# Raw weights of an attention and MLP kernel: two tiles of a chunk and two assembled ones, or six of half a chunk converted in place

## Chip, core and metric

The kernel runs on one core of one Trainium2 chip. The metric is the device time of one execution in microseconds (us), the median of three runs. The core has five instruction streams that are named by their engines: PE (TensorE, matmuls), DVE (VectorE), ACT (ScalarE), POOL (GpSimd) and SP (SyncE, which here only asks for DMA transfers). ACT also asks for some transfers, in the same stream as its arithmetic.

## What is computed

Top-k attention over 4 batches of 8 heads, 576 positions and a head size of 64, then two MLPs on all 2304 tokens.

```python
scores = scale * np.matmul(q, k.transpose(0, 1, 3, 2))
kth = np.partition(scores, -32, axis=-1)[..., -32:-31]
scores = np.where(scores >= kth, scores, -1000000000.0)
attn = softmax(scores)                      # exp(s - max) / (sum + 1e-09)
x = matmul(attn, v)                         # to [2304, 512]
...
h = np.maximum(x @ w_in, 0.0)               # 512 -> 2048
x = h * h @ w_out                           # 2048 -> 512
...
h = x @ w_in2
out = np.maximum(0.01 * h, h) @ w_out2
```

The kernel gets q, k, v and the weights as 64-bit words; it makes fp32 values of them itself. For matmuls it splits each operand into a high and a low part and sums three products (high by high, high by low, low by high).

## The kernel before

**Attention** keeps DVE busy: per row tile four rounds of MAX8 and MATCH_REPLACE8 find the 32nd largest score (L928, L930). ACT makes exponentials and copies banks of PSUM, POOL does the low parts, PE scores, transposes and products.

**The MLPs** work on blocks of 512, 256, 384, 512, 256 and 384 tokens. A phase is one block in one layer, and has 16 steps; step f uses chunk f of the layer's weights: 512 words of w_in and 512 of w_out in each of 128 partitions, as 64-bit words 1 MB. Per step PE makes h (12 matmuls, L653), ACT `ga` and `gh` (L663, L664 in layer 0; L670, L672 in layer 1), POOL the low part `gl`, and PE adds to `acc` (12 matmuls of 512 columns, L690 or L692).

**Fresh chunks.** In the first phase of each layer (32 steps, both for block 0) a chunk comes from the inputs. `w_raw` loads it (L522, SP) into a raw tile of 8 KB a partition (tag `wraw`, two tiles). `w_convert` turns it into fp32, two steps ahead of its use, in the pieces that STAGES spreads over a step: ACT takes the low 32-bit words of the whole chunk to a tile of their own, `wc` (L543; 4 KB a partition, two tiles), then for each half ACT moves the scaled high words to a bank of PSUM with Prelu, whose large slope for negative numbers marks the sign (L552), DVE shifts and ORs them into `wc` (L559), ACT copies the result as the high part to `wi` or `wo` (L563), and POOL subtracts for the low part (L564). `w_store` writes `wi` and `wo` to DRAM for the later phases (two transfers per chunk, SP), which read them back with `w_load`. The raw tile is free once both halves were marked, `wc` once POOL has subtracted.

**Chunks 0 and 1** are loaded and prepared early, by `lead_passes` (low words L583 at 26 to 30 us, high words L584) and `lead_bits` at the end of block 0's attention. They use Copy for the high words, and so a second DVE operation for the sign (L590, L591).

**Output.** At the end of a layer-1 phase ACT copies each `acc` to a tile `y` (L708; same tag and two tiles as `wc`), and asks for the transfers to the output (L710) in its own queue. Block 5's input takes the two `wraw` tiles.

**Order.** A scheduler sets each engine's order from the order in which the program writes the instructions and from priorities (`high_priority`, `behind`); tiles of a tag are handed out in turn or as they come free, and whoever writes a tile waits for the readers of what stood in it. Of the MLPs, `run_moe` runs quanta of three matmuls between the attention's slots.

Of the kernel before, what the change touches and what calls it, by code (L numbers as in the profile page):

```python
# [57 lines left out]
WRB = 2  # L58
WCB = 2
# [28 lines left out]
def topk_attention_moe_moe2_kernel(  # L88
# [323 lines left out]
    def block_x(blk):  # L412

        if "x" not in blk:
            i = SETS[blk["idx"]]
            m = max(x["n"] for x in blocks if SETS[x["idx"]] == i)
            if i == 2:
                ts = [pool.tile([P, 2, 2, m], R, tag="wraw", name="x2", bufs=WRB) for _ in range(NK // 2)]
                blk["x"] = [(t[:, i, 0], t[:, i, 1]) for t in ts for i in range(2)]
# [96 lines left out]
    def w_raw(i):  # L516
        if i >= len(steps) or not fresh[i]:
            return
        _, layer, f = steps[i]
        if W64:  # L520
            t = pool.tile([P, 1024, 2], U, tag="wraw", name="wraw", bufs=WRB)
            SP.dma_start(t.rearrange("p c t -> p (c t)"), WS[layer][f].bitcast(U))  # L522
        else:
            t = pool.tile([P, 1024], F, tag="wraw", name="wraw", bufs=WRB)
            SP.dma_start(t, WS[layer][f])
        wraw[i] = t
# [9 lines left out]
    def w_convert_steps(i):  # L536
# [4 lines left out]
        if W64:  # L541
            b = pool.tile([P, 1024], U, tag="wc", name="wc", bufs=WCB)
            ACT.activation(b, raw[:, :, 0], AF.Copy, scale=L_SCALE, bias=L_BIAS)  # L543
            c = b.bitcast(F)
        else:
            c = raw
        v = [None, None]

        def high(x):
            if W64:  # L550
                v[x] = bank()
                ACT.activation(v[x], raw[:, x * 512:x * 512 + 512, 1].bitcast(F), AF.Prelu, scale=H_SCALE,  # L552
                               alpha=2.0 ** 32)

        def bits(x):
            if W64:
                vu, bx = v[x].bitcast(U), b[:, x * 512:x * 512 + 512]
                with behind("dve"):
                    DVE.scalar_tensor_tensor(bx, vu, 3, bx, op0=OP.logical_shift_left, op1=OP.bitwise_or)  # L559

        def parts(x):
            w, cx = w2[x], c[:, x * 512:x * 512 + 512]
# [11 lines left out]
    def lead_passes(i):  # L574
        led[i] = []
        raw = wraw.pop(i)
        c = pool.tile([P, 1024], U, tag="wc", name="wc", bufs=WCB)
        for x, w in enumerate(w_alloc(i)):
            xs = slice(x * 512, x * 512 + 512)
            lo, hi, b = raw[:, xs, 0], raw[:, xs, 1], c[:, xs]  # L580
# [423 lines left out]
```

## Time and profile before

| | us |
|---|---|
| median of three runs | 1190.59 (1190.24 to 1194.26) |
| the profiled execution | 1191.68 |
| its span in the trace | 1189.9 |
| busy: PE, DVE, ACT, POOL | 1127.2, 840.9, 818.9, 748.5 |

The rows further down are of that profiled execution, 1.1 us above the median. Starts are counted from the start of the span. In square brackets a timeline gives how long an engine sat idle before an instruction, and what released it. The stretches are: attention alone to 165 us; to 195 the step over to the first MLP block; to 395 the two fresh phases, with a seam between the layers at 300 to 330; then phases that reload their weights, with attention beside them to about 930; then MLPs alone.

### The profile page before, as it was taken

The numbers are of one execution on the slowest core, as the hardware profiler recorded it, in microseconds if no ns is written. First come the engines' busy times: TensorE is split into PE (matmuls) and PEld (weight loads), VectorE is DVE, ScalarE is ACT, GpSimd is POOL, SyncE is SP. The second block draws the span as 40 slices with busy tenths as digits, with TensorE's granted clock in tenths as the row PEclk, the third lists the DMA queues.
The fourth block names the chain that finished last, engine by engine and source line by source line (L and its number), as shares of the span: only waits on it lengthen the run. The fifth ranks groups of instructions, "written<-read, shape, count | busy, mean of one in ns | idle before, by whom it ended". The sixth has DMA issues, their size and how long they took to land.

```text
span 1189.9 us, 20032 instructions
## 1 busy us (share of the span) xinstructions
PE 1127.2 (95%) x6376; PEld 991.7 (83%) x6376; DVE 840.9 (71%) x1771; ACT 818.9 (69%) x1823; POOL 748.5 (63%) x960
## 2 busy tenths in 40 slices
PE   5898977999899999999999999999999999999997
PEld 4777766778678899999998997888788899999996
DVE  7999998766775759999999998999998100110010
ACT  6999988998989768877776776566866433333322
POOL 7968747999779677677897766777756443002100
PEclk9899989999899999999999998999999999999999
DMA  9868757998999697899897886777675499779973
GB/s 311 281 215 284 255 196 259 383 344 309 328 349 331 211 349 269 281 330 384 303 307 255 302 297 231 224 238 229 201 238 184 158 333 323 259 247 346 352 260 120
DMA packets 108201, 329.53 MB, mean 277 GB/s; under 512 B 17216, under 2 KB 25408, under 8 KB 104000
## 3 DMA queue, kind: packets, MB, share of 16 engines
q1 hardware_dynamic: 105472, 323.53, 79.1%
q10 hardware_dynamic: 2624, 4.72, 1.1%
q8 instruction: 52, 0.85, 0.3%
q14 instruction: 53, 0.43, 0.1%
HBM read 257.03 MB, written 71.17 MB: 276 GB/s over the span
## 4 chain that ended last, share of the span: by engine, by line
PE 73%; ACT 11%; DVE 8%; DMA 4%; issue 2%; POOL 2%; SPq 0%; ACTq 0%; POOLq 0%; DVEq 0%
PE h L653 30%; PE acc L692 16%; PE acc L690 13%; PE att L447 5%; DVE m L928 4%; PE att L350 3%; DVE w L930 3%; PE att L436 2%; ACT e L333 2%; PE att L310 1%; PE sp L310 1%; ACT s L311 1%; ACT stage L311 1%; ACT e L329 1%; DMA out_dram<-y 1%
## 5 line engine op out<-in xcount | busy, mean ns | idle before, releaser
L653 PE MATMUL h<-xh,wi 128*128 128x512 f32 (+2 forms) x1280 | 348.1, 346 | 6.0 <-ACT xh L704 2.8
L928 DVE MAX8 m<-w 128x8 f32<-128x576 f32 x432 | 312.8, 749 | 2.4
L653 PEld LDWEIGHTS h<-xh,wi 128*128 128x128 f32 x1280 | 228.6, 192 | 31.2 <-ACT ga L663 3.3
L673 POOL TENSOR_TENSOR gl<-ga,gh 128x512 fp32r<-128x512 f32 (+2 forms) x160 | 162.6, 1019 | 131.4 <-ACT gh L672 109.7
L930 DVE MATCH_REPLACE8 w<-m,w 128x576 f32<-128x576 f32 x288 | 213.3, 743 | 0.4
L653 PE MATMUL h<-xl,wi 128*128 128x512 f32 (+2 forms) x640 | 206.3, 342 | 0.0
L358 POOL TENSOR_TENSOR PTs<-whole,PTs 128x512 fp32r<-128x512 f32 x112 | 144.5, 1297 | 59.8 <-ACT whole L357 58.2
L690 PE MATMUL acc<-gh,wo 128*128 128x512 f32 (+2 forms) x768 | 156.9, 344 | 1.6 <-ACT y L708 0.8
L692 PE MATMUL acc<-wo,gh 128*128 128x512 f32 x576 | 152.5, 397 | 0.2 <-ACT gh L672 0.2
L690 PEld LDWEIGHTS acc<-gh,wo 128*128 128x128 f32 x768 | 128.2, 191 | 14.2 <-ACT gh L664 1.3
L329 ACT ACTIVATE e<-s,m 128x576 f32<-128x576 f32 x144 | 112.1, 781 | 39.8 <-DVE m L928 29.3
L653 PEld LDWEIGHTS h<-xl,wi 128*128 128x128 f32 x640 | 120.8, 190 | 10.7
L928 DVE MAX8 m<-s 128x8 f32<-128x576 f32 x144 | 104.3, 748 | 30.9 <-ACT s L311 28.5
L673 DVE TENSOR_TENSOR gl<-ga,gh 128x384 fp32r<-128x384 f32 x32 | 17.9, 559 | 151.2 <-ACT gh L672 148.5
L670 ACT ACTIVATE ga<-h 128x512 f32<-128x512 f32 (+2 forms) x96 | 46.5, 490 | 111.3 <-PE h L653 111.0
L692 PEld LDWEIGHTS acc<-wo,gh 128*128 128x128 f32 x576 | 105.1, 188 | 20.5 <-ACT gh L672 0.4
L333 ACT ACTIVATE e<-e,nb 128x576 f32<-128x576 f32 x144 | 111.5, 778 | 3.0 <-POOL nb L323 2.6
L930 DVE MATCH_REPLACE8 w<-m,s 128x576 f32<-128x576 f32 x144 | 107.0, 744 | 0.5
L350 PE MATMUL att<-ident,e 128*128 128x128 f32 x576 | 87.8, 277 | 7.7 <-ACT e L333 6.2
L447 PE MATMUL att<-PTs,VT 128*128 128x256 f32 (+2 forms) x504 | 89.4, 301 | 5.5 <-ACT whole L357 1.9
L665 POOL TENSOR_TENSOR ga<-ga 128x512 f32<-128x512 f32 (+2 forms) x80 | 66.4, 831 | 42.5 <-ACT gh L664 41.9
L345 POOL TENSOR_SCALAR e<-e,rc 128x576 f32<-128x576 f32 x112 | 83.0, 753 | 14.0 <-DVE rc L341 11.4
(100 smaller groups left out, 2070.3 us busy)
## 6 DMA issues: line engine op xcount, KB each, us to landing
wi<-wd SPq DMA_DIRECT2D x160, 512.0 KB, 5.2
wo<-wd SPq DMA_DIRECT2D x160, 512.0 KB, 5.2
wraw<-in_w_dram SPq DMA_DIRECT2D x32, 1024.0 KB, 7.6
sd<-stage SPq DMA_DIRECT2D x76, 288.0 KB, 3.0
s<-sd SPq DMA_DIRECT2D x76, 288.0 KB, 4.9
wd<-wi SPq DMA_DIRECT2D x32, 512.0 KB, 6.9
wd<-wo SPq DMA_DIRECT2D x32, 512.0 KB, 7.1
vd<-VT SPq DMA_DIRECT2D x16, 640.0 KB, 6.9
```

The costliest lines, as they stand in the source:

```text
L329: ACT.activation(t["e"], t["s"], AF.Prelu, bias=pr["m8"][:, i, 31:32], scale=-1.0, alpha=1.0 / FAR)
L333: ACT.activation(e, e, AF.Exp, bias=pr["nb"][:, i:i + 1], scale=-FAR, accum_out=pr["sum"][:, i:i + 1])
L345: POOL.tensor_scalar(e, e, pr["rc"][:, i:i + 1], 1.0, op0=OP.mult, op1=OP.mult)
L350: PE.transpose(ps[:, j * P:(j + 1) * P], t["e"][:, j * P:(j + 1) * P], ident)
L358: POOL.tensor_tensor(pts[:, 4:8, c:c + P], whole, pts.bitcast(F)[:, 0:4, c:c + P], op=OP.subtract)
L447: PE.matmul(ps, lhsT=l, rhs=r, start=i == 0, stop=i == len(mm) - 1)
L653: PE.matmul(two[r][:, 0:n], lhsT=ws[r][:, w, c * P:(c + 1) * P], rhs=x[c][y][:, 0:n], start=cnt == mine[0], stop=cnt == mine[-1])
L673: (DVE if j >= GLD else POOL).tensor_tensor(gl[:, 0:n], a[:, 0:n], gh.bitcast(F)[:, 0:n], op=OP.subtract)
L690: PE.matmul(acc[c][:, 0:n], lhsT=wo[:, w, cs], rhs=g[:, 0:n], start=first, stop=last)
L692: PE.matmul(acc[c], lhsT=g[:, cs], rhs=wo[:, w, :], start=first, stop=last)
L928: cur["dve"] = DVE.max(out=m8[:, x, 8 * r:8 * r + 8], in_=t["s"] if r == 0 else t["w"])
L930: cur["dve"] = DVE.match_replace(out=t["w"], in_to_replace=m8[:, x, 8 * r:8 * r + 8], in_values=t["s"] if r == 0 else t["w"], imm_value=NEG)
```

## The change

Raw tiles hold half a chunk (512 words, 4 KB a partition), and there are six (`WRB = 6`); a chunk's load is two transfers of 512 KB. The low words are converted in place, in the even 32-bit words of the raw tile, one instruction of 512 for each half instead of one of 1024 for both; DVE ORs in place, and the high copy and POOL's subtraction read the even words, at a step of 8 bytes. `wc` is gone, and the room in SBUF is the same (24 KB a partition). Chunks 0 and 1 are marked with Prelu as well, so the second DVE operation goes. `y` lies in the raw tiles, two `acc` to a tile; block 5's input lies in four of them. A chunk is stored in the step that first uses it, before in the step ahead of it.

```diff
-WRB = 2
-WCB = 2
+WRB = 6
...
-                ts = [pool.tile([P, 2, 2, m], R, tag="wraw", name="x2", bufs=WRB) for _ in range(NK // 2)]
+                ts = [pool.tile([P, 2, m], R, tag="wraw", name="x2", bufs=WRB) for _ in range(NK)]
...
-            t = pool.tile([P, 1024, 2], U, tag="wraw", name="wraw", bufs=WRB)
-            SP.dma_start(t.rearrange("p c t -> p (c t)"), WS[layer][f].bitcast(U))
...
+        wraw[i] = []
+        for x in range(2):
+                t = pool.tile([P, 512, 2], U, tag="wraw", name="wraw", bufs=WRB)
+                SP.dma_start(t.rearrange("p c t -> p (c t)"), WS[layer][f].bitcast(U)[:, x * 1024:x * 1024 + 1024])
...
+            wraw[i].append(t)
...
+    def mark(dst, t):
+        ACT.activation(dst, t[:, :, 1].bitcast(F), AF.Prelu, scale=H_SCALE, alpha=2.0 ** 32)
+
+    def low_bits(t):
+        ACT.activation(t[:, :, 0], t[:, :, 0], AF.Copy, scale=L_SCALE, bias=L_BIAS)
+
+    def put_together(t, v):
+        b = t[:, :, 0]
+        DVE.scalar_tensor_tensor(b, v.bitcast(U), 3, b, op0=OP.logical_shift_left, op1=OP.bitwise_or)
...
-            b = pool.tile([P, 1024], U, tag="wc", name="wc", bufs=WCB)
-            ACT.activation(b, raw[:, :, 0], AF.Copy, scale=L_SCALE, bias=L_BIAS)
...
+                low_bits(raw[x])
                 v[x] = bank()
-                ACT.activation(v[x], raw[:, x * 512:x * 512 + 512, 1].bitcast(F), AF.Prelu, scale=H_SCALE,
-                               alpha=2.0 ** 32)
+                mark(v[x], raw[x])
...
-            ACT.activation(b, lo, AF.Copy, scale=L_SCALE, bias=L_BIAS)
-            ACT.activation(v, hi.bitcast(F), AF.Copy, scale=H_SCALE)
-            led[i].append((b, v.bitcast(U), w))
+            low_bits(t)
+            mark(v, t)
+            led[i].append((t, v, w))
...
-                DVE.scalar_tensor_tensor(b, vu, 3, b, op0=OP.logical_shift_left, op1=OP.bitwise_or)
-                DVE.scalar_tensor_tensor(b, vu, 0x80000000, b, op0=OP.bitwise_and, op1=OP.bitwise_or)
...
+                put_together(t, v)
...
-                w_store(si + 1)
+                w_store(si)
...
-                y = pool.tile([P, 1024], F, tag="wc", name="y", bufs=WCB)[:, 0:512]
+                if c % 2 == 0:
+                    both = pool.tile([P, 2, 512], F, tag="wraw", name="y", bufs=WRB)
+                y = both[:, c % 2]
...
-    at(rslot[0] - 1, w_store, 0)
```

The order of instructions moves at three places that matter below.

ACT where block 0's attention ends. `wraw_2330` and `wraw_2340` are chunks 2 and 3 in the kernel before; `xh0_671` is the high part of block 0's MLP input, its last writer is the row with `xn_2551`; `e0`, `e1` are exponentials of the next tiles. Before:

```order
L543 ACTIVATE wc_2569<-wraw_2330 128x1024
L360 ACTIVATE PT_115<-att_2489 128x4x128
L378 ACTIVATE PT_115<-att_2495 64x256
L468 ACTIVATE xh0_671<-xn_2463 64x256
L329 ACTIVATE e0_107<-s2_103,m8_2506 128x576
L401 ACTIVATE rb_2443<-att_2495 64x256
L311 ACTIVATE s4_105<-att_2531 128x288
L468 ACTIVATE xh0_671<-xn_2551 64x256
L543 ACTIVATE wc_2638<-wraw_2340 128x1024
L329 ACTIVATE e1_108<-s3_104,m8_2506 128x576
L333 ACTIVATE e0_107,sum_2507<-e0_107,nb_2750 128x576
```

Now, where `wraw_2345` and `wraw_2347` are the halves of chunk 3, and `wraw_2625` the first half of chunk 4:

```order
L536 ACTIVATE wraw_2345<-wraw_2345 128x512
L377 ACTIVATE PT_115<-att_2497 64x256
L359 ACTIVATE PT_115<-att_2491 128x4x128
L328 ACTIVATE e0_107<-s2_103,m8_2508 128x576
L536 ACTIVATE wraw_2347<-wraw_2347 128x512
L310 ACTIVATE s4_105<-att_2531 128x288
L400 ACTIVATE rb_2449<-att_2497 64x256
L536 ACTIVATE wraw_2625<-wraw_2625 128x512
L328 ACTIVATE e1_108<-s3_104,m8_2508 128x576
L332 ACTIVATE e0_107,sum_2509<-e0_107,nb_2755 128x576
L467 ACTIVATE xh0_671<-xn_2551 64x256
L332 ACTIVATE e1_108,sum_2509<-e1_108,nb_2755 128x576
```

Three conversions of low words (L536) now stand ahead of the last `xh0` row; before, the one that stood nearest came behind it. Chunk 2's are further ahead, since its halves are loaded at the start of the program.

SP's queue at the same place (`wd0_0`, `wd0_1`: the stores of chunks 0 and 1; `sd`: scores put aside in DRAM; `vraw`: a load of the attention). Before:

```order
L314 DMA sd143_2278<-stage_2257 128x576
L522 DMA wraw_2330<-in_w1_dram 128x2048
L522 DMA wraw_2340<-in_w1_dram 128x2048
L600 DMA wd0_0_116<-wi_2312 128x1024
L601 DMA wd0_0_116<-wo_2313 128x1024
L600 DMA wd0_1_117<-wi_2351 128x1024
L249 DMA vraw_2826<-in_v_dram 128x640
L601 DMA wd0_1_117<-wo_2352 128x1024
```

Now, `wraw_2625` and `wraw_2627` being chunk 4's halves:

```order
L313 DMA sd143_2282<-stage_2261 128x576
L523 DMA wraw_2345<-in_w1_dram 128x1024
L604 DMA wd0_0_116<-wi_2315 128x1024
L523 DMA wraw_2347<-in_w1_dram 128x1024
L605 DMA wd0_0_116<-wo_2316 128x1024
L523 DMA wraw_2625<-in_w1_dram 128x1024
L604 DMA wd0_1_117<-wi_2357 128x1024
L523 DMA wraw_2627<-in_w1_dram 128x1024
L605 DMA wd0_1_117<-wo_2358 128x1024
```

The half loads of chunks 3 and 4 are interleaved with the stores of chunks 0 and 1, which give back their raw tiles.

ACT at the end of the program, before:

```order
L670 ACTIVATE ga<-h 128x384
L672 ACTIVATE gh<-ga 128x384
L708 ACTIVATE y<-acc 128x512 x2
L710 DMA out_dram<-y 64x512 x2
L710 DMA out_dram<-y 128x512
L708 ACTIVATE y<-acc 128x512
L710 DMA out_dram<-y 128x512
```

and now:

```order
L674 ACTIVATE ga<-h 128x384
L676 ACTIVATE gh<-ga 128x384
L714 ACTIVATE y<-acc 128x512 x3
L716 DMA out_dram<-y 64x512 x2
L716 DMA out_dram<-y 128x512 x2
```

All three copies to `y` now stand ahead of the four transfers.

## Rows read from the trace of the kernel before

**Rows 1.** Busy time by stretch (columns in its first line)

```profile
core 0: us, PE busy (x) PEld busy (x) DVE busy (x) ACT busy (x) POOL busy (x), PEclk, DMA share, GB/s
30.00:165.00 135.00, 121.85 (x716) 100.22 (x716) 133.88 (x291) 125.17 (x351) 102.39 (x155) 0.98 0.73 246
165.00:195.00 30.00, 21.21 (x89) 15.54 (x90) 25.73 (x54) 24.37 (x58) 15.23 (x22) 0.86 0.61 214
195.00:395.00 200.00, 190.02 (x869) 153.54 (x869) 139.34 (x266) 181.57 (x340) 178.40 (x175) 0.96 0.94 338
210.00:270.00 60.00, 56.81 (x271) 46.03 (x270) 43.83 (x83) 57.93 (x111) 58.57 (x60) 0.98 0.98 359
600.00:800.00 200.00, 194.58 (x1056) 173.21 (x1055) 193.07 (x419) 138.12 (x293) 145.41 (x186) 0.97 0.80 266
```

**Rows 2.** The page, part 4: the chain that ended last

```profile
PE 73%; ACT 11%; DVE 8%; DMA 4%; issue 2%; POOL 2%; SPq 0%; ACTq 0%; POOLq 0%; DVEq 0%
```

**Rows 3.** ACT timeline, two places: start us, us, what, [idle before]

```profile
730.63 0.60 ACT L708 ACTIVATE y<-acc 128x512 f32<-128x512 f32 x1 [1.94 <-DMA out_dram<-y]
...
1182.46 1.08 ACT L708 ACTIVATE y<-acc 128x512 f32<-128x512 f32 x2 [2.68 <-PE acc L692]
1183.08 1.77 ACTq L710 DMA_DIRECT2D out_dram<-y  x3
1186.16 0.60 ACT L708 ACTIVATE y<-acc 128x512 f32<-128x512 f32 x1 [2.62 <-DMA out_dram<-y]
1186.79 0.34 ACTq L710 DMA_DIRECT2D out_dram<-y  x1
```

**Rows 4.** PE timeline, two places, columns as in 3

```profile
732.26 0.41 PE L447 MATMUL att<-PTs,VT 128*128 128x320 f32 x1 [1.95 <-ACT whole L357]
...
960.17 0.50 PE L690 MATMUL acc<-gh,wo 128*128 128x256 f32 x2 [0.82 <-ACT y L708]
```

**Rows 5.** Groups on ACT, 195:395: xcount | busy, mean ns | idle before

```profile
L552 ACT ACTIVATE att<-wraw 128x512 f32<-128x512 f32 x58 | 36.0, 632 | 7.2 <-DMA wraw<-in_w_dram 7.0
L543 ACT ACTIVATE wc<-wraw 128x1024 uint32<-128x1024 uint32 x28 | 31.8, 1137 | 0.0
```

**Rows 6.** Operations on wc: ns min/median/max, first and last start

```profile
L564 POOL TENSOR_TENSOR wi<-wc,wi x30: 1278/1299/1321, 197.8 to 388.4; 128x512 fp32r<-128x512 f32 x30
...
L583 ACT ACTIVATE wc<-wraw x4: 682/704/722, 26.2 to 29.7; 128x512 uint32<-128x512 uint32 x4
...
L591 DVE SCALAR_TENSOR_TENSOR wc<-v,wc x4: 671/676/680, 172.9 to 179.9; 128x512 uint32<-128x512 uint32 x4
```

**Rows 7.** ACT timeline where the first MLP block begins

```profile
184.37 0.41 ACT L468 ACTIVATE xh<-xn 64x256 fp32r<-64x256 f32 x1
...
191.47 1.08 ACT L663 ACTIVATE ga<-h 128x512 f32<-128x512 f32 x2
...
200.77 0.64 ACT L552 ACTIVATE att<-wraw 128x512 f32<-128x512 f32 x1 [0.84 <-DMA wraw<-in_w_dram]
```

**Rows 8.** POOL timeline of the same place

```profile
180.40 1.27 POOL L593 TENSOR_TENSOR wi<-wc,wi 128x512 fp32r<-128x512 f32 x1
```

**Rows 9.** The chain in order of time, 190:262: start, us, what

```profile
193.99 6.76 DMA wraw<-in_w_dram
...
206.56 4.61 PE h L653 x12
...
241.85 2.76 PE h L653 x12
```

**Rows 10.** The page, part 6: DMA issues, KB, us to landing

```profile
wi<-wd SPq DMA_DIRECT2D x160, 512.0 KB, 5.2
...
wraw<-in_w_dram SPq DMA_DIRECT2D x32, 1024.0 KB, 7.6
```

**Rows 11.** ACT timeline, a later wait for a raw chunk

```profile
338.68 0.65 ACT L552 ACTIVATE att<-wraw 128x512 f32<-128x512 f32 x1 [2.60 <-DMA wraw<-in_w_dram]
```

**Rows 12.** Waits of PE, 206:400: us in total, times, longest

```profile
PE h L653 <- ACT ga L670: 0.6, 1, 0.6
```

More of the change, by code (lines that the diff above doesn't have):

```diff
@@ L417, in block_x @@
             if i == 2:
-                ts = [pool.tile([P, 2, 2, m], R, tag="wraw", name="x2", bufs=WRB) for _ in range(NK // 2)]
-                blk["x"] = [(t[:, i, 0], t[:, i, 1]) for t in ts for i in range(2)]
+                ts = [pool.tile([P, 2, m], R, tag="wraw", name="x2", bufs=WRB) for _ in range(NK)]
+                blk["x"] = [(t[:, 0], t[:, 1]) for t in ts]
             else:
@@ L540, in w_convert_steps @@
         raw = wraw.pop(i)
-        if W64:
-            b = pool.tile([P, 1024], U, tag="wc", name="wc", bufs=WCB)
-            ACT.activation(b, raw[:, :, 0], AF.Copy, scale=L_SCALE, bias=L_BIAS)
-            c = b.bitcast(F)
-        else:
-            c = raw
         v = [None, None]
@@ L550, in high @@
             if W64:
+                low_bits(raw[x])
                 v[x] = bank()
-                ACT.activation(v[x], raw[:, x * 512:x * 512 + 512, 1].bitcast(F), AF.Prelu, scale=H_SCALE,
-                               alpha=2.0 ** 32)
+                mark(v[x], raw[x])
         def bits(x):
             if W64:
-                vu, bx = v[x].bitcast(U), b[:, x * 512:x * 512 + 512]
                 with behind("dve"):
-                    DVE.scalar_tensor_tensor(bx, vu, 3, bx, op0=OP.logical_shift_left, op1=OP.bitwise_or)
+                    put_together(raw[x], v[x])
         def parts(x):
-            w, cx = w2[x], c[:, x * 512:x * 512 + 512]
+            w, cx = w2[x], low_word(raw[x])
+            cx = cx.bitcast(F) if W64 else cx
             ACT.activation(w[:, 0, :], cx, AF.Copy)
@@ L575, in lead_passes @@
         led[i] = []
[L576 to L580, printed above, removed]
+        for t, w in zip(wraw.pop(i), w_alloc(i)):
             v = stage_psum.tile([P, 512], F, tag="sd" if len(led) == 2 and not led[i] else "sp", name="v",
                                 bufs=SDB if len(led) == 2 and not led[i] else SPB)
-            ACT.activation(b, lo, AF.Copy, scale=L_SCALE, bias=L_BIAS)
-            ACT.activation(v, hi.bitcast(F), AF.Copy, scale=H_SCALE)
-            led[i].append((b, v.bitcast(U), w))
+            low_bits(t)
+            mark(v, t)
+            led[i].append((t, v, w))
     def lead_bits(i):
-        for b, vu, w in led.pop(i):
+        for t, v, w in led.pop(i):
             with behind("recip" if i else "shift"):
-                DVE.scalar_tensor_tensor(b, vu, 3, b, op0=OP.logical_shift_left, op1=OP.bitwise_or)
-                DVE.scalar_tensor_tensor(b, vu, 0x80000000, b, op0=OP.bitwise_and, op1=OP.bitwise_or)
-            split_hi(w[:, 0, :], b.bitcast(F))
-            POOL.tensor_tensor(w[:, 1, :], b.bitcast(F), w.bitcast(F)[:, 0, :], op=OP.subtract)
+                put_together(t, v)
+            c = low_word(t).bitcast(F)
+            split_hi(w[:, 0, :], c)
+            POOL.tensor_tensor(w[:, 1, :], c, w.bitcast(F)[:, 0, :], op=OP.subtract)
     def w_store(i):
```

11 lines of the change are left out of this document (6 added, 5 removed).

## The prediction

> **What bounds the kernel now.** I read the busy times by stretch first, then the chain, then the timelines at the places that the change touches. No one engine bounds the whole: up to 165 us DVE is busy 133.88 of 135, from 600 to 800 it is busy 193 of 200, and between them the MLPs decide [rows 1]. The chain that ended last is 73% PE, 11% ACT, 8% DVE and 4% DMA [rows 2], so what the change does to ACT and to transfers can only count where PE is made to wait. There are two such stretches. From 165 to 195, the step over to the first MLP block, PE does 21.21 of 30 us at a clock of 0.86. From 195 to 395, the fresh phases that convert weights, PE works 190.02 of 200, ACT 181.57, POOL 178.40, and the DMA engines 0.94; in 210 to 270 ACT and POOL are at 57.93 and 58.57 of 60 [rows 1]. All parts of the change but `y` lie in those two.
>
> **The change part by part.** The sum is made against the profiled execution, 1191.68 us, and put on the median at the end.
>
> *A, the end.* Now the third `y` waits 2.62 us for an output transfer to free its tile, starts at 1186.16, and its transfer is asked for at 1186.79, after which nothing else is left [rows 3]. With two `acc` to a tile and six tiles, the third copy follows the second, which ends at 1182.46 + 1.08 = 1183.54, and by the order the four requests come behind it. The first can be asked for when the first copies are done, about 1183.6; three requests took 1.77 us, 0.59 each with their waits, and a lone one 0.34 [rows 3]. Between these the fourth is asked for at 1184.6 to 1185.4; with some 0.5 each it is 1185.1 to 1185.2, so 1186.79 - 1185.2 = **-1.6** (-2.2 to -0.8; -2.6 if nothing of the wait came back).
>
> *B, `y` in the middle.* The same wait stands at 730.63 with 1.94 us on ACT, and PE behind it waits 1.95 for `whole`, which ACT makes next; the other is at 960, where PE waits 0.82 for `y` itself [rows 3, 4]. Both waits go. At 960 only MLPs run, so I count 0.8 in full. At 730 DVE sets the pace (193.07 of 200 [rows 1]), and a stall of PE there is mostly made up; I take a third, 0.6. **-1.4** (-2.8 to 0).
>
> *C, the step over.* Removed: four DVE operations of 0.676 us (L591) on the chunks 0 and 1 [rows 6]. Of this I worked out from the order which DVE instructions stand ahead of the low part of the block's last input: eight shift-and-or fewer before, four in their place, and one MAX8 and one MATCH_REPLACE8 of the next tiles more, net some 1.2 us less. Moved against it: ACT's conversions. Before, the last `xh` copy (184.37) stood ahead of the nearest conversion of low words [rows 7]; now three half conversions stand ahead of it, and the last is that of chunk 4's first half. Its raw tile is one that chunk 0 or 1 gave back, so its load waits for a POOL subtraction: that of chunk 1's `wi` ended at 180.40 + 1.27 = 181.7 [rows 8], and with the DVE work gone may end about 1.5 earlier, 180.1. A transfer of 512 KB lands 5.2 us after its request [rows 10]: 185.3, and 0.7 for the conversion gives `xh` near 186 to 188 in place of 184.4. What is queued behind that wait on ACT is `xh`, and behind `xh` PE's matmuls on the second half of the block's columns; PE has 14 h matmuls of the other columns and 6 of scores ahead of those by the order, over 4 us at 2.76 / 12 = 0.23 each [rows 9]. So `ga`, at 191.47 now [rows 7], stays where it is within 1 us. Behind it the change gains. In the kernel before the chain runs through a raw chunk that is asked for at 193.99 and takes 6.76; ACT waits for it until 200.77, and the h of step 3 begins only at 206.56, its 12 matmuls at 4.61 us against 2.76 later on, nearer the half clock [rows 7, 9]. In the new order chunks 2 and 3 are loaded and passed earlier, and that h can begin some 3 us earlier; the step after it then waits an estimated 1.7 for chunk 5, whose tiles also come back from POOL, and POOL's work up to there is the same. I take **-2.5** (-4.9: all of the 3 and more of the clock; +3: the wait for chunk 4 is a transfer late and hits PE).
>
> *D, ACT's added work.* Low words of half a chunk cost 704 ns (L583 [rows 6]), those of a whole one 1137 [rows 5]: 2 x 704 - 1137 = 271 ns more per chunk, for 28 chunks in 195 to 395: 7.6 us. ACT is idle 18.4 of these 200, of which 7.0 are waits for raw chunks [rows 1, 5]. So it fits on the whole, and PE has 10 us of idleness in which to be late. Not everywhere: in 210 to 270 ACT is idle 2.07 and would get 60/200 of 7.6 = 2.3 more, while POOL is fuller still and gets nothing. I take **+1** (0 to +7.6). The cover is POOL, which ends each chunk later than ACT; if ACT becomes the later one the whole 7.6 counts (a rival below).
>
> *E, loads.* Six half tiles against two whole ones, but a raw tile is now held until POOL has subtracted, before only until ACT had marked the chunk. By following which tile follows which in the order, 13 of the 54 half loads have less than 8 us of ACT's rows (7.0 in the mean) between the high copy that precedes them in their tile and their own conversion; they need POOL's lag behind ACT (an estimate of 2.8), the request, and 5.2 to land [rows 10], some 8.3. That leaves 13 x 1.3 = 17 us of waiting on ACT at the most, against 7.0 now [rows 5]. Such a wait reaches PE weakly: 2.60 us at 338.68 came through as 0.6, PE's one wait for `ga` of L670 [rows 11, 12]. So 10 more on ACT are 2.3 on PE at that rate. Against it, the half that is needed first now lands 2.4 us sooner after its request (7.6 - 5.2), and most half loads have more time than they need, where each of the whole ones waits for the chunk before it. **+0.5** (-0.6 to +5). The Trainium skill, page "DMA: Bandwidth & Descriptors", section "Rules for kernel authors", asks for 128 partitions and at least 1 MiB per transfer, which speaks against halves: by it two halves would land 10.4 us after the first request, 2.8 later than the 7.6 of the whole, E would be about +2.5 and the sum 2 higher. No row here has two such halves back to back; the single 512 KB transfers do move less per us (98 KB) than the whole ones (135 KB).
>
> *F, the step of 8 bytes.* ACT, DVE and POOL now read, two of them also write, every second word. ACT's reads of raw tiles (L543, L552) already have that step and L552 costs 632 ns like dense copies [rows 5], so 0; for POOL and DVE no row has it, and the nearest, POOL's dense subtraction, is 1299 ns [rows 6]: between 0 and a rival below. The later stores stay off every chain: SP's requests only follow others, and `wd` is read a phase later. 0.
>
> Sum: -1.6 - 1.4 - 2.5 + 1 + 0.5 = -4.0, 1187.7 on the profiled execution, which lies 1.1 above the median: **1186.6**. The bounds of the terms that move alone give 1182.5 to 1190 for this case.
>
> **The rivals.** *R1, the steps stay ahead.* With chunks 0 to 2 loaded at the start and six tiles, ACT's 7.0 us of raw waits go [rows 5] and the fresh phases run at PE's pace. For it: PE's idle 10 of 200 and the half clock after 195 [rows 1, 9]. Against it: POOL at 58.57 of 60 isn't relieved. It gives A + B + C at -4.9, and some -3 of the 10: about -11, 1180.
>
> *R2, ACT takes over the bound, slower.* In 195 to 395 ACT's added 7.6 us all land on the path, with 3 of raw waits, less 3 for A and B: +7.6, 1198.2. It decides where ACT's idle time between due conversions is less than what is added: in 210 to 270 that is 2.07 against 2.3, so there it is already so; at the other places ACT has 16.3 of idle time in 140. For it: two of the three engines in the loop are full, and ACT's waits are also why `wc` came late to DVE. Against it: POOL is the fuller.
>
> *R3, strided operands cost.* If POOL's 64 subtractions took half as long again, 0.65 x 60 in the fresh phases = 39 us against POOL's idle 21.6 [rows 1, 6]: +17 less 4, 1204 and up. The Trainium skill, page "GPSIMD Engine Reference", section 7, puts such a 50% on reads with a step over 8 bytes; the step here is 8 exactly, and by that rule the time is the forecast's. No row before has POOL at that step.
>
> *R4, nothing moves.* The scheduler's order gives the seam back and DVE's attention makes up B: only A, less D, 1190.
>
> **How the numbers follow.** Forecast 0.52, R1 0.20, R2 0.18, R3 0.06, R4 0.04. Some 0.5%, 6 us, is what a measurement of this kernel can tell from no change: 1184.6 to 1196.5 counts as the same. Of the forecast's 0.52, 0.18 are below; R1 is all below; of R2 0.15 are above, 0.03 within; R3 is above, R4 within. Faster 0.38, same 0.41, slower 0.21. The range takes R1 in down to 1179 and R2 up to 1199.5; R3, the far end of R2 and a larger gain than R1 are left out, near 0.2.
>
> **What would show it.** A: no wait before the last `y`, last request by 1185.5 counted back by what was gained before. B: no idle time ended by an output transfer at 730 and 957. C: `ga` of the first step at 191 to 192.5, step 3's h near 203. D and E: ACT busy 187 to 189 in the fresh phases, its raw waits under 17 us, PE still at 188 or more of 200. F: L540 at 0.68 us, L572 at 1.30. Wrong it is if the first ACT wait ahead of `xh` lasts over 3 us, if PE's work of the fresh phases stretches past 400, or if POOL's 1.30 grows.

## The result and the profile after

The changed kernel takes 1201.97 us (1199.58 to 1204.12); the kernel before, run beside it, 1191.16. The ratio of their runs is 1.0076 (95% interval 1.0057 to 1.0096): some 9 us slower (the medians are 10.8 apart), where the prediction said 1186.6, with a range up to 1199.5, and put 0.21 on slower by more than 0.5%. The profiled execution took 1204.12 us, its span 1201.9.

The busy times of the same stretches as in [rows 1]:

```profile
core 0: us, PE busy (x) PEld busy (x) DVE busy (x) ACT busy (x) POOL busy (x), PEclk, DMA share, GB/s
30.00:165.00 135.00, 117.80 (x675) 95.74 (x675) 127.43 (x274) 120.80 (x337) 98.67 (x150) 0.95 0.72 244
165.00:195.00 30.00, 25.36 (x108) 18.74 (x109) 25.82 (x54) 22.95 (x57) 16.61 (x21) 0.83 0.61 200
195.00:395.00 200.00, 183.50 (x844) 146.11 (x843) 139.50 (x267) 184.56 (x370) 175.52 (x175) 0.98 0.92 327
210.00:270.00 60.00, 54.05 (x248) 43.03 (x247) 45.30 (x88) 56.43 (x113) 56.46 (x58) 0.97 0.97 360
600.00:800.00 200.00, 196.00 (x1091) 176.63 (x1090) 197.63 (x429) 138.67 (x296) 148.91 (x188) 0.99 0.81 270
```

Three things stand out. TensorE does 183.50 us of work in the fresh phases against 190.02, though ACT is not fuller where it was fullest (56.43 of 60 in 210 to 270, before 57.93), so ACT has not become the bound. The stretch ahead of 165 us, in which hardly anything was changed, is poorer too: DVE 127.43 of 135, before 133.88. And 600 to 800 is better: DVE 197.63 against 193.07.

The profile's page, part 4 (the chain of work that ended last); before, the chain was 73% PE [rows 2], and the page named no store of weights (`wd`) among its lines:

```profile
PE 50%; DVE 16%; ACT 4%; DMA 4%; POOL 2%; issue 2%; ACTq 0%; SPq 0%; POOLq 0%; DVEq 0%
PE h L657 23%; PE acc L696 13%; PE acc L694 8%; DVE m L933 8%; DVE w L935 6%; PE att L446 3%; DMA wd<-wi 2%; PE att L349 2%; DMA wi<-wd 1%; ACT e L328 1%; DMA wraw<-in_w_dram 1%; DVE PTs L374 1%; POOL gl L677 1%; DVE xf L452 1%; ACT whole L356 0%
```

`DMA wd<-wi`, the stores of w_in's parts, now hold 2% of the span (the shares sum to 78%, so a part of this chain isn't accounted for). The end of the program, with the columns of [rows 3]:

```profile
1195.76 1.08 ACT L714 ACTIVATE y<-acc 128x512 f32<-128x512 f32 x2 [2.68 <-PE acc L696]
1196.38 0.49 ACTq L716 DMA_DIRECT2D out_dram<-y  x1
1196.73 0.60 ACT L714 ACTIVATE y<-acc 128x512 f32<-128x512 f32 x1
1196.92 1.73 ACTq L716 DMA_DIRECT2D out_dram<-y  x3
```

The wait of 2.62 us is gone, and from the start of the first of these copies to the end of the span it is 1201.9 - 1195.76 = 6.1 us, before 1189.9 - 1182.46 = 7.4.

ACT where the first MLP block begins, answering to [rows 7]:

```profile
185.57 0.68 ACT L536 ACTIVATE wraw<-wraw 128x512 uint32<-128x512 uint32 x1 [1.05 <-DMA wraw<-in_w_dram]
188.19 0.68 ACT L536 ACTIVATE wraw<-wraw 128x512 uint32<-128x512 uint32 x1 [0.54 <-DMA wraw<-in_w_dram]
191.75 0.41 ACT L310 ACTIVATE s<-att 128x288 f32<-128x288 f32 x1 [2.89 <-PE att L309]
...
193.85 0.68 ACT L536 ACTIVATE wraw<-wraw 128x512 uint32<-128x512 uint32 x1 [1.28 <-DMA wraw<-in_w_dram]
195.96 0.41 ACT L467 ACTIVATE xh<-xn 64x256 fp32r<-64x256 f32 x1
...
199.77 0.60 ACT L667 ACTIVATE ga<-h 128x512 f32<-128x512 f32 x1
```

The last `xh` stands at 195.96 in place of 184.37, behind three waits for half loads (1.05, 0.54, 1.28) and one of 2.89 for PE; `ga` at 199.77 in place of 191.47. The groups on ACT that answer to [rows 5], and under them POOL's subtraction, answering to [rows 6], each with the columns given there:

```profile
L536 ACT ACTIVATE wraw<-wraw 128x512 uint32<-128x512 uint32 x55 | 37.0, 673 | 7.4 <-DMA wraw<-in_w_dram 7.1 <-POOL sum L339 0.3
L571 ACT ACTIVATE wi<-wraw 128x512 fp32r<-128x512 f32 x30 | 20.1, 670 | 0.8 <-DVE wraw L540 0.8
```

```profile
L572 POOL TENSOR_TENSOR wi<-wraw,wi x30: 1305/1324/1385, 205.5 to 399.2; 128x512 fp32r<-128x512 f32 x30
```

The half loads land in 6.2 us in the median, the whole ones took 7.6 [rows 10].

### The profile page after: what moved, and what is told of

Its sections match the earlier page's. It is cut to its first block, busy times and chain, and to the rows that moved or that the text cites. A ratio compares the mean times of both kernels' runs of the same rounds, so it can differ in the third digit from the quotient of the medians.

```text
span 1201.9 us, 20154 instructions
## 1 busy us (share of the span) xinstructions
PE 1131.5 (94%) x6376; PEld 989.1 (82%) x6376; DVE 841.0 (70%) x1767; ACT 821.4 (68%) x1853; POOL 749.2 (62%) x960
## 4 chain that ended last, share of the span: by engine, by line
PE 50%; DVE 16%; ACT 4%; DMA 4%; POOL 2%; issue 2%; ACTq 0%; SPq 0%; POOLq 0%; DVEq 0%
PE h L657 23%; PE acc L696 13%; PE acc L694 8%; DVE m L933 8%; DVE w L935 6%; PE att L446 3%; DMA wd<-wi 2%; PE att L349 2%; DMA wi<-wd 1%; ACT e L328 1%; DMA wraw<-in_w_dram 1%; DVE PTs L374 1%; POOL gl L677 1%; DVE xf L452 1%; ACT whole L356 0%
## 5 line engine op out<-in xcount | busy, mean ns | idle before, releaser
L349 PE MATMUL att<-ident,e 128*128 128x128 f32 x576 | 91.2, 281 | 10.5 <-ACT e L332 8.2
L694 PE MATMUL acc<-gl,wo 128*128 128x512 f32 (+2 forms) x384 | 87.7, 347 | 3.3 <-POOL gl L677 3.1
L349 PEld LDWEIGHTS att<-ident,e 128*128 128x128 f32 x576 | 70.2, 143 | 23.3 <-ACT e L332 13.8
```

Source lines behind the costliest of these rows:

```text
L349: PE.transpose(ps[:, j * P:(j + 1) * P], t["e"][:, j * P:(j + 1) * P], ident)
L694: PE.matmul(acc[c][:, 0:n], lhsT=wo[:, w, cs], rhs=g[:, 0:n], start=first, stop=last)
```

## The experiments

Three theories came from these rows. **S**: the later store costs. **T**: a raw tile that is held until POOL has subtracted makes loads late. **O**: the order of the attention, which the scheduler shuffled from the first conversions at 25 us on, costs ahead of 165 us. Beside them the prediction's rival R2, here called **theory A** (not its term A): ACT's added work. **ST** is S and T together: the late store costs where SP is held up by raw loads. Ratios are against the kernel before, run beside each kernel on the same chip; 0.001 is 1.2 us.

A warning that holds for all of them: an edit can also change the order of instructions far from its place. In the traces, PE, DVE and ACT run the very same order in the kernel before and e2, and in e6 and e7; in the other pairs compared below the orders part. So a difference between two such kernels shows what the edit is worth in this program, not by itself by which path.

To see where time goes I also count: "the 800th MLP matmul" is the 800th of the 4320 matmuls of `h` and `acc`, in order of time, which falls just behind the fresh phases; MAX8 instructions (576) count the attention.

### e1: stores a step ahead again, in the changed kernel

```diff
-                w_store(si)
+                w_store(si + 1)
...
+    at(rslot[0] - 1, w_store, 0)
```

> The changed kernel with one part undone: chunk si+1 is stored in step si again (and chunk 0 ahead of the first step). Theory S (the later store): a store of wi has to land before the tile of wi, one of three, takes the chunk three further on, and asked for a step later it lands too late; the chain of the changed kernel passes four times through a wi store of 5.8 to 7.3 us in 280 to 356. Then about 6 of the 10.8 us come back: 1194 to 1197, no wi store on the chain. Theory T (raw tiles are held until POOL's subtraction, so loads and what is queued behind them on SP come late): at most 2 back, 1199 to 1202. Theory O (the order of the attention was shuffled ahead of 165 us, where VectorE is 7 us behind before the first step): that lag stays in either case, and the time stays above 1197.

Measured: 1193.89 us, ratio 0.9998 (0.9980 to 1.0017). The 9 us are gone with the stores' place alone, as S expected; T and O had expected a longer time. In the changed kernel the chain passes four times through such a store (in e1 once still, for 6.4 us), as in these pieces (start us, us, what):

```profile
280.17 0.33 SPq L523
...
280.56 5.96 DMA wd<-wi
...
300.30 1.37 POOL wi L572
...
301.68 0.33 SPq L523
...
302.07 5.81 DMA wd<-wi
...
307.90 0.67 ACT wi L571
```

POOL ends a subtraction at 301.67, which frees a raw tile; SP asks for the raw load (L523) that waited for it, and only then for the store queued behind it, which lands 5.8 us later; ACT's high copy to that `wi` tile (L571) starts when it has landed. But this is no idle time: ACT was busy up to 307.90 with other instructions, and in 165 to 400 us the changed kernel's engines sit idle for such a store only here:

```profile
POOL wi L572 <- DMA wd<-wi: 0.6, 1, 0.6
```

Nor is the time lost there. The 800th MLP matmul, behind the last fresh chunk, starts at 433.4 us in the changed kernel and at 435.5 in e1, so the changed kernel is ahead there; the 1200th starts at 517.9 and 510.4. Busy times of 500 to 520 us, in the changed kernel and in e1:

```profile
500.00:520.00 20.00, 17.06 (x116) 15.06 (x116) 19.74 (x43) 16.21 (x42) 10.82 (x15) 1.00 0.62 190
```

```profile
500.00:520.00 20.00, 20.00 (x140) 18.75 (x141) 19.81 (x45) 17.54 (x45) 11.91 (x17) 1.00 0.84 289
```

The two orders part at 194 us on ACT, 200 on DVE and 215 on PE. So the late store's 9 us are shown, but not that they are a wait for its landing; that they come by the order, in the phases behind, is a rival that no run here separates.

VectorE's lag ahead of 165 us stayed: up to there it has done 148.78 us of work, in the changed kernel 150.50, before 156.97. (The expectations name the same lag as 7 us, read from the place of a MAX8 instruction.)

### e2: later stores alone, in the kernel before

```diff
-                w_store(si + 1)
+                w_store(si)
...
-    at(rslot[0] - 1, w_store, 0)
```

> The kernel before with one part of the change alone: the stores asked for at first use. The order of the other instructions is the same up to the second phase. Theory S: 4 to 8 us slower, 1195 to 1199, with wi stores on the chain. Theory T: the stores stand behind raw loads that wait for marks of ACT and not for POOL, so little happens: 1190 to 1193. Theory O: 1190 to 1192.

Measured: 1192.86 us, 0.9991 (0.9970 to 1.0011). There the later store costs nothing measurable, and every engine keeps its order. So S is not a price of its own: it needs something else that the change brought.

### e4: ACT's half instructions alone, in the kernel before

```diff
-            ACT.activation(b, raw[:, :, 0], AF.Copy, scale=L_SCALE, bias=L_BIAS)
...
+                ACT.activation(b[:, xs], raw[:, xs, 0], AF.Copy, scale=L_SCALE, bias=L_BIAS)
                 v[x] = bank()
```

> The kernel before with one part of the change alone: the low words converted in two instructions of half a chunk, each ahead of its mark, in tiles of their own as before. Theory A (ACT's added work, 271 ns per chunk, is on the path in the fresh phases): 5 to 8 us slower, 1196 to 1199. Theories S and T: within 2 us of before. Theory O (any edit shuffles the attention's order and costs or gives some us by it): a shift of VectorE by some us at 165 us already, ahead of any fresh chunk.

Measured: 1192.71 us, 0.9988 (0.9969 to 1.0007). Theory A falls: there the added 0.2 to 0.3 us per chunk cost nothing that can be measured, where it expected 5 to 8 us.

### e6: not in place, later stores kept

```diff
-WRB = 6
+WRB = 4
+WCB = 4
...
-        ACT.activation(t[:, :, 0], t[:, :, 0], AF.Copy, scale=L_SCALE, bias=L_BIAS)
+        b = pool.tile([P, 512], U, tag="wc", name="wc", bufs=WCB)
+        ACT.activation(b, t[:, :, 0], AF.Copy, scale=L_SCALE, bias=L_BIAS)
...
-                    both = pool.tile([P, 2, 512], F, tag="wraw", name="y", bufs=WRB)
-                y = both[:, c % 2]
+                y = pool.tile([P, 512], F, tag="wc", name="y", bufs=WCB)
```

> The changed kernel with one part undone: the low words go to tiles of their own again (four of half a chunk, beside four raw tiles of half a chunk; y in those tiles, one acc each), so that a raw tile is free once it is marked. ACT's work, half loads and later stores stay. Theory T: 5 or more us back, 1193 to 1197, and SP's raw loads no longer wait for POOL (84 us of such waits in 195 to 400 in the changed kernel). Theory S: the wi stores still come late, 1198 to 1202; theory A: 1198 to 1202.

Measured: 1181.54 us, 0.9891 (0.9860 to 0.9922): 13 us faster than the kernel before, and 22 faster than the changed one, with its later stores. T had expected 1193 to 1197 us. Room is the same 24 KB.

### e7: the same with stores a step ahead

> The kernel of e6 (raw tiles free at the mark) with the stores asked for a step ahead again, which fills the square of in place or not by late or early store. Theory ST (the two parts hurt together: a late store stands on SP behind raw loads that wait for POOL): with raw tiles free early the store's time is of no account, so like e6, 1180 to 1184. If the late store costs by itself whatever stands ahead of it, some 5 us faster than e6, 1175 to 1178.

Measured: 1182.64 us, 0.9906 (0.9889 to 0.9924). With raw tiles free at the mark the place of the store is of no account (and the engines' orders in e6 and e7 are the same); with raw tiles held it is worth 9 us (e1 against the changed kernel). What SP's raw loads waited for in 195 to 400 us (total, times, longest), in the changed kernel and in e7:

```profile
SPq L523 <- POOL wi L572: 45.3, 20, 6.5
SPq L523 <- POOL wo L572: 38.3, 14, 5.0
```

```profile
SPq L524 <- ACT wc L538: 44.9, 27, 4.5
SPq L524 <- ACT att L534: 11.2, 10, 2.8
```

SP stands 84 us before raw loads that wait for POOL's last step, and everything behind them stands too; in e7 the loads wait for ACT's first steps, 56 us in these two lines (and the early stores wait another 45 for POOL). So SP stands in either kernel; what differs is whom it waits for.

### e3: two `acc` to a tile of `y`, alone, in the kernel before

```diff
-                y = pool.tile([P, 1024], F, tag="wc", name="y", bufs=WCB)[:, 0:512]
+                if c % 2 == 0:
+                    both = pool.tile([P, 1024], F, tag="wc", name="y", bufs=WCB)
+                y = both[:, c % 2 * 512:c % 2 * 512 + 512]
```

> The kernel before with one part of the change alone: two acc to a tile of y, so four outputs can be under way in the two tiles. By the prediction's A and B 2 to 4 us faster than before; if the stretch 716 to 774, which the kernels with more room for y pass 6 to 9 us sooner, owes that to y, 6 or more faster. If the transfers of y were hidden, the same as before within 1.5.

Measured: 1182.97 us, 0.9906 (0.9886 to 0.9926): 11 us from this edit, as much as all of e7 gives. So more room for `y` is enough for the whole gain, and half loads, half conversions and Prelu together add nothing measurable to it. Where, show the busy times of the kernel before (columns as in the first rows of this section's profile) and its PE timeline behind the wait of [rows 4]:

```profile
730.00:745.00 15.00, 12.12 (x43) 9.71 (x42) 10.89 (x25) 9.30 (x19) 9.33 (x11) 0.77 0.54 172
745.00:760.00 15.00, 15.00 (x76) 12.32 (x75) 14.93 (x34) 10.66 (x21) 11.47 (x14) 1.00 0.70 227
```

```profile
733.61 2.23 PE L447 MATMUL att<-PTs,VT 128*128 128x320 f32 x7 [0.94 <-POOL PTs L358]
735.65 0.63 PE L653 MATMUL h<-xh,wi 128*128 128x512 f32 x1
```

and the same stretch in e3:

```profile
730.00:745.00 15.00, 15.00 (x74) 12.48 (x73) 14.87 (x33) 9.07 (x19) 11.71 (x14) 1.00 0.83 284
745.00:760.00 15.00, 15.00 (x75) 12.49 (x74) 14.80 (x33) 10.73 (x23) 10.03 (x13) 1.00 0.72 227
```

Before, PE waits 1.95 and 0.94 us here, and then runs at a granted clock of 0.77: a matmul of 512 columns at 735.65 has 0.43 us to the next one (736.07), where it takes 0.23 at full speed. DVE is busy 10.89 of 15 us, so it loses 4 us; in e3 it loses 0.13. Counted by MLP matmuls, e3 is 2.2 us behind the kernel before at the 2160th (723.0 us before) and 3.1 ahead at the 2240th (750.5): 5.3 us come from this place. Some 3 more come by the 2800th (916.6, e3 910.4), in the attention's last stretch, and 1.3 at the end of the program. The orders of the two kernels part from 418 us on, so for those 3 us, and in part for the others, a better order is a rival that isn't excluded.

### e5: Prelu for chunks 0 and 1 alone, in the kernel before

```diff
-            ACT.activation(v, hi.bitcast(F), AF.Copy, scale=H_SCALE)
+            ACT.activation(v, hi.bitcast(F), AF.Prelu, scale=H_SCALE, alpha=2.0 ** 32)
...
-                DVE.scalar_tensor_tensor(b, vu, 0x80000000, b, op0=OP.bitwise_and, op1=OP.bitwise_or)
```

> The kernel before with one part of the change alone: chunks 0 and 1 marked with Prelu, four DVE operations of 0.68 us fewer. By the prediction's C 1 to 2.5 us faster, with the first h of the MLPs 1 to 2 us ahead of before. If the order's shuffle decides more than the operations saved, any value within 4 us of before, and VectorE's place at 165 us shows it.

Measured: 1190.04 us, 0.9973 (0.9950 to 0.9996), some 3 us; the first h starts at 179.9 us, before at 183.5 (in e2, which has the order of the kernel before, at 186.0, so single executions differ by 2.5 here).

### e10: later stores asked for by ACT, in the changed kernel

```diff
-        SP.dma_start(d[:, 0:2, :], wi.bitcast(F))
-        SP.dma_start(d[:, 2:4, :], wo.bitcast(F))
+        ACT.dma_start(d[:, 0:2, :], wi.bitcast(F))
+        ACT.dma_start(d[:, 2:4, :], wo.bitcast(F))
```

> The changed kernel with its later stores asked for by ACT in place of SP, so that they no longer stand behind raw loads that wait for POOL. Theory ST: most of what the earlier store gave comes back without an earlier store, 1192 to 1197, no wi store on the chain. Theory S alone (a step later is too late by itself): 1199 to 1203. If ACT's requests cost (some 60 of them at 0.3 to 0.6 us where ACT is over nine tenths busy), 1200 and more with a fuller ACT in 195 to 395.

Measured: 1217.92 us, 1.0191 (1.0162 to 1.0219). It did not tell what it was to tell. The stores no longer stand behind raw loads, but the raw loads themselves have become the chain, one behind the other:

```profile
302.26 1.34 POOL wi L572
...
303.61 7.14 DMA wraw<-in_w_dram
...
310.78 0.69 ACT wraw L536
...
313.49 7.47 DMA wraw<-in_w_dram
...
320.99 0.67 ACT wraw L536
```

The first waits for the subtraction above it, the second is asked for behind another transfer; each lands 7 us later, and ACT's conversion starts as it lands. ACT isn't fuller, as the expectation's last case had it: it is busy 180.13 of 195 to 395, in the changed kernel 184.56. Why the loads are later here than in the changed kernel is open.

### e11 and e12: six tiles, two of them kept back until the first MLP step

```diff
+    def hold_raw():
+        for _ in range(2):
+            t = pool.tile([P, 512, 2], U, tag="wraw", name="wraw", bufs=WRB)
+            POOL.memset(t[:, 0:8, 0], 0)
...
+    at(184, hold_raw)
+    at(rslot[0] - 31, give_raw)
```

e11 has early stores, e12 late ones.

> The kernel of e1 (in place, stores a step ahead) with two of its six raw tiles kept back until shortly before the first MLP step: POOL writes eight numbers to each early, and eight more then. Chunk 2 is then not loaded at the start, and the attention's order is that of e7 for 400 instructions of VectorE and TensorE. Theory O (the in-place kernels lose 7 us in the attention by the order that the early third chunk brings): VectorE is back at 156 us for its 120th MAX8 in place of 165, and the time 4 to 8 us under that of e1: 1186 to 1190. Theory T (held raw tiles cost it all, in the fresh phases): VectorE is back but the time stays with e1, 1191 to 1195, and against e7 the loss comes after 195 us.

> The changed kernel with two raw tiles kept back like that, stores late. Theory O: 4 to 8 us under the changed kernel, 1194 to 1198, and 8 to 10 above e11, the price of the late stores where raw tiles are held. Theory T: 1199 to 1204, VectorE back at 165 us and the loss made again in the fresh phases, with wi stores and raw loads on the chain.

Measured: e11 1189.09 us, 0.9966 (0.9942 to 0.9990); e12 1202.49, 1.0074 (1.0046 to 1.0103). The order agrees with e7's over 296 instructions of VectorE, to 146 us, and 736 of TensorE (the 400 of the expectation was too much for VectorE). e11 is 4 us under e1, as little as O allows, though the intervals overlap; VectorE's work up to 165 us is 152.22 us, so only 3.4 of the lag are back, and the 120th MAX8 starts at 162.2 us, not at O's 156. The late store costs 13 us here (e12 against e11). This pair has its loss in the fresh phases: the 320th MLP matmul starts at 288.7 us in e11 and 293.6 in e12, the 800th at 425.6 and 440.0, and behind that, where the orders of PE, DVE and ACT are the same again, the distance stays. e12 shows no gain from the attention's order over the changed kernel, so O isn't confirmed by that pair.

### e13 to e16: five tiles; a fourth `wi` tile; early or late stores

```diff
-WRB = 6
+WRB = 5
...
-        wi = pool.tile([P, 2, 512], R, tag="wi", name="wi", bufs=3)
+        wi = pool.tile([P, 2, 512], R, tag="wi", name="wi", bufs=4)
```

e13 has the first hunk alone, e14 both, e15 the first and early stores, e16 both and early stores.

> The changed kernel with five raw tiles of half a chunk in place of six; a base for the next two, which need the room. Fewer raw tiles that are held until POOL's subtraction make raw loads later still: if the hold is what costs (theory T), 5 or more us slower than the changed kernel, 1205 to 1215; if not, about the same, 1199 to 1204.

> The kernel of e13 with a fourth tile of wi in the room that the fifth raw tile left, stores late. Theory W (a late store costs because it has to land before one of the three wi tiles is written again): 8 to 13 us faster than e13, and no wi store on the chain. Theory H (it costs by standing among the raw loads in SP's queue): as slow as e13 within 3 us, since the queue's contents stay.

> The kernel of e13 with the stores a step ahead. Theories W and H: 8 to 13 us faster than e13, under W about level with e14. If the price of late stores was one of the order of instructions in the changed kernel alone, within 4 us of e13.

> The kernel of e15 (five raw tiles, stores a step ahead) with a fourth tile of wi. If the fourth tile gained 7 us in e14 because late stores have to land before a wi tile is written again, it has nothing to gain where stores are early: 1187 to 1192 as e15, ratio 0.996 to 0.999. If it gained by reloading chunks earlier in the later phases, whatever the stores do, some 5 to 8 us faster again: 1181 to 1185, ratio 0.990 to 0.993.

| ratio to before | three `wi` tiles | four |
|---|---|---|
| late stores | e13: 1.0033 (1.0016 to 1.0051) | e14: 0.9974 (0.9956 to 0.9991) |
| early stores | e15: 0.9974 (0.9956 to 0.9993) | e16: 0.9981 (0.9964 to 0.9998) |

(1195.58, 1189.12, 1189.74 and 1190.88 us.) The fourth tile takes back the whole price of the late store, 7 us (W expected 8 to 13), and gains nothing where stores are early. So the late store's price depends on the number of `wi` tiles, as theory W says (a `wi` tile can't be written again before its store has landed), and not as H says (the store stands among the raw loads in SP's queue), which expected e14 to stay as slow as e13. That the price is a wait for the landing isn't shown: the 2160th MLP matmul starts at 730.7 us in e13 and 730.2 in e14, far behind the last late store, and the 6 us are lost later, most of them in 940 to 980 us, where TensorE does 35.25 us of work in e13 and 39.84 in e14. Their orders part at 314 us on ACT, 326 on PE and 332 on DVE; that the fourth tile helps by another order is a rival that stands. And five tiles are faster than six (e13 against the changed kernel, by 5 us), against the expectation of T for e13.

### e17: in place in the MLPs alone

```diff
-WRB = 6
+WRB = 4
+WCB = 4
...
-            low_bits(t)
-            mark(v, t)
-            led[i].append((t, v, w))
+            b = pool.tile([P, 512], U, tag="wc", name="wc", bufs=WCB)
+            ACT.activation(b, t[:, :, 0], AF.Copy, scale=L_SCALE, bias=L_BIAS)
+            mark(v, t)
+            led[i].append((b, v, w))
```

> In place for the 30 chunks that are converted in the MLPs alone: chunks 0 and 1 and y go to four tiles of half a chunk of their own, beside four raw tiles of half a chunk; stores a step ahead. The order of every engine is that of e7 up to the end of block 0's attention (257 rows of VectorE, 590 of TensorE, 376 of ACT). Theory O (in place costs by what it does to the attention ahead of 165 us, since chunks 0 and 1 lie in the raw tiles from 25 us on): close to e7, 1181 to 1185, ratio 0.990 to 0.994. Theory T (it costs by raw tiles held until POOL's subtraction in the fresh phases, and here only four of them): 1191 or more, ratio above 0.998, with ACT's waits for raw loads over 15 us in 195 to 400.

Measured: 1194.68 us, 1.0014 (1.0002 to 1.0026): 13 us slower than e7, with e7's order up to 175 us and its work of VectorE at 165 (157.13 us, e7 156.93): here the price is T's, not O's, though the orders part behind that and another order can have a share. With four held tiles the price is 13 us, with five 8 (e15), with six of which two come late 7 (e11). ACT's wait for raw loads in 195 to 400 us, in e17 (T expected over 15) and in e7:

```profile
ACT wraw L537 <- DMA wraw<-in_w_dram: 12.4, 14, 2.6
```

```profile
ACT att L534 <- DMA wraw<-in_w_dram: 0.8, 1, 0.8
```

These waits aren't the whole path: in e15 they are only 1.7 us, and yet it is 8 us slower than e7. And it is the attention that comes late out of the fresh phases, not the MLPs: the 800th MLP matmul starts at 422.1 us in e17 and 421.7 in e7, but the 300th MAX8 at 545.1 and 532.9. What VectorE waited for in 195 to 400 us, in e17, where it stands 58.5 us for ACT's conversions of raw words, and in e7, where it stands 34.5:

```profile
DVE wraw L541 <- ACT att L534: 58.5, 32, 6.4
```

```profile
DVE wc L542 <- ACT wc L538: 27.4, 17, 2.8
...
DVE wc L542 <- ACT att L534: 7.1, 6, 3.7
```

The MLPs lose their time behind that: their 1400th matmul starts at 549.8 us in e17 and 538.1 in e7. Busy times of 395 to 600 us, in e17 and in e7:

```profile
395.00:600.00 205.00, 198.81 (x1390) 186.97 (x1389) 183.06 (x395) 154.54 (x369) 150.95 (x205) 1.00 0.86 307
```

```profile
395.00:600.00 205.00, 203.28 (x1430) 193.92 (x1430) 185.16 (x402) 153.81 (x366) 153.80 (x213) 1.00 0.87 308
```

## Why the prediction was wrong

**The sum of what the runs showed.** `y` gives 11 us (e3). In place with early stores takes them back (e1 at 0.9998 against e7 at 0.9906). The late store on top of it costs 9 (1.0076 against 0.9998). The parts do not add up in all places (Prelu's 3 us of e5 are not seen on top of e3 in e7), but these three make the result. Which edits cost and gain is shown; by which path the last two cost is open in part (below). The prediction's range also came out too narrow for its own terms: their bounds, added, run from 1180 to 1205 us, not from 1182.5 to 1190 as it has it.

**A held.** The end is 7.4 - 6.1 = 1.3 us shorter, for a predicted 1.6.

**B had the right place, and its size was some seven times too small.** I took 0.6 for the wait at 730 as a third of PE's 1.95, and 0.8 for that at 960. e3 gives 11 in all, so some 9 to 10 beside A. The step that failed is "a stall of PE there is mostly made up". It wasn't: DVE was stalled as well, 4 us in 15, PE ran the next matmuls at near half clock, and the MLPs gain 5.3 us at this place alone when the wait is gone. The busy times of 730 to 745 show both and could have been read before. The rest of the 9 to 10 comes elsewhere, and in part perhaps by the order that changed with the edit.

**C failed in its place.** I let `xh` wait to 186 to 188 and `ga` stay within 1 us of 191.47; they came at 195.96 and 199.77. ACT's waits for the half loads are there, 2.9 us in three, where I had reckoned with one. But VectorE was already 6.5 us late at 165 us (150.50 us of work against 156.97). What it waited for in 80 to 165 us, now:

```profile
DVE m L933 <- ACT s L310: 3.0, 3, 2.1
DVE xn L466 <- ACT rb L400: 2.6, 2, 2.3
DVE m L933 <- POOL nb L322: 1.0, 1, 1.0
```

and before:

```profile
DVE m L928 <- ACT s L311: 0.4, 1, 0.4
```

I compared the order only at the places that the change touches, and took the attention's as given. The three kernels that share this order (the changed one, e1, e10) have 148.78 to 150.50 us of VectorE's work done at 165 us, the other in-place ones 151.64 to 152.93, e17 and those with tiles of their own for the low words 154.65 to 157.13. How much of that reaches the end is not settled: e11 against e1 says 4 us, e12 against the changed kernel none. TensorE's work of the fresh phases, 183.50, is also under the 188 that I had named.

**D held.** L536 takes 673 ns in place, so 2 x 673 - 1137 = 209 ns more per chunk and not 271; ACT's busy time in the fresh phases rose by 3.0 us, and e4 has no price for it.

**E had the right place and the wrong path.** ACT's waits for raw loads are 7.1 us, as before, not 17; so far the reckoning was even too dark. But the in-place hold costs 7 to 13 us with early stores (e11, e15, e1 and e17 against e7), where E stood at +0.5: I priced only ACT's waits, and not that VectorE waits behind them for ACT's conversions (24 us longer in e17 than in e7), nor what stands behind the raw loads in SP's queue. My rate for what reaches PE was also a guess: the wait of 0.6 that I set beside the one at 338.68 stands at 346.88. The Trainium skill, page "DMA: Bandwidth & Descriptors", section "Rules for kernel authors", asks for at least 1 MiB per transfer, which spoke against the halves; e7 with halves is level with e3 with whole chunks (0.9906 both), so no price of them shows here (in e7 a half lands in 6.6 us in the median, in e3 a whole chunk in 8.2).

**F: one half held, the other decided the sign.** The step of 8 bytes costs little: POOL's subtraction 1.32 us for 1.30, ACT's copies 670 ns for 631, together 60 x 0.02 on POOL and 60 x 0.04 = 2.4 us on ACT. The Trainium skill, page "GPSIMD Engine Reference", section "Performance pitfalls for Q7 kernels", puts its penalty on steps above 8 bytes, and the trace agrees. The sentence that failed is the next one: "The later stores stay off every chain: SP's requests only follow others, and `wd` is read a phase later. 0." I asked who reads what is stored, and not who writes the tile that is stored from. `wi` has three tiles, and the chunk three further on is written to the same one; a store lands in 7.3 us in the median. The runs showed +9 in its place: moving the stores back takes 9 us away (e1), and with five raw tiles a fourth `wi` tile takes away the 7 that the late stores cost there (e14). In e2 and e6, with raw tiles free early, the late store is free. Whether its price is a late landing or the order that the scheduler made with a tile that comes free later stays open: idle time put down to a late store is 0.6 us in the changed kernel.

**The rivals.** Two lay on the slower side, and that they came near is luck. R2 had 1198 for a reason that was wrong: by its own test ACT's idle time in 210 to 270 should have been used up, and it is 3.57 us where it was 2.07. R3's 1204 comes nearest to the measured 1201.97, but POOL's subtraction took 1.32 us, not half as long again. No rival named the lifetime of a `wi` tile.

**What stays open.** In 165 to 400 us the engines wait 0.6 us for late stores in the changed kernel, none in e13 and 2.8 in e12. Only e12 loses its time where the stores are; in the changed kernel and in e13 it is lost behind the fresh phases. So the timed kernels show that the late store costs with three `wi` tiles and raw tiles held, but not the path. A late store in a kernel whose order is kept by hand would tell. How the price of in place splits into T and O with six tiles, and e10's slowness, are not explained either.

## What to carry to other kernels

When a store is moved or a conversion is made in place, list for each tile who may write it next and what must have happened by then; in place keeps a load's tile until the last step, and the next load can't be asked for before. A short wait in a stretch where two engines are full can cost more than its length: read the busy times and the clock of the 15 us behind it. Where a scheduler sets the order, compare the whole order of two kernels, not only the places of the edit, before a difference is put down to a wait. And test parts of a bundle apart: here one small part gains 11 us, and without the in-place conversion the rest is as fast (e3 1183 us, e6 1181.5).

## What the runs showed of the hardware

An idle time of 1.95 and 0.94 us on TensorE, 0.4 us of work between them, was followed by matmuls at 0.43 us in place of 0.23, and a granted clock of 0.77 over 730 to 745; the stall of under 2 us that I had priced at 0.6 was worth some 5 us in the MLPs at this place. Reading every second 32-bit word added 2% to POOL's subtraction (1.32 us for 1.30) and 6% to ACT's copies (670 ns for 631).
